# Local attention: outputs of two items in one PSUM tile, scores in alternation with transpositions

## The chip, the cores and the metric

The kernel runs on one core of a Trainium2 chip. The metric is the device time of one execution in microseconds (us); the median of several runs counts. Engines are called by the names of the profile: PE is TensorE (matmuls and transpositions), DVE is VectorE, ACT is ScalarE, SP is the engine whose queue issues the DMAs here.

## The reference

Three steps follow one another: local attention with a few global tokens, then two MLPs. There are 4 batches of 8 heads of width 64, 512 local and 32 global positions.

```python
s_g = scale * q_g @ k_all.T;  out_g = sm(s_g) @ v_all        # 32 global queries see all 544 keys
s_ll = where(abs(i - j) <= 32, scale * q_l @ k_l.T, -1e9)    # local queries: a band of +-32
a_l = sm(concat([scale * q_l @ k_g.T, s_ll]))                # and the 32 global keys
out_l = a_l @ concat([v_g, v_l])
x = out.transpose(0, 2, 1, 3).reshape(B * S, 512)            # 2176 tokens
h = x @ w_in;  x = where(h >= 1, h, where(h <= -1, 0, (h + 1)**2 / 4)) @ w_out    # 512 -> 2048 -> 512
y = ((x @ w_a) * (x @ w_b)) @ w_out2                         # 512 -> 1536 -> 512
```

## The kernel before

**Tiles.** The 2048 local tokens are 16 blocks of 128, the 128 global ones a 17th. `TILES` groups them by three into tiles 0 to 4; tile 5 has block 15 and the global block. The first MLP takes one tile (384 columns) after the other.

**Attention items.** A `Local` item is one block and one pair of heads; there are 64, four for each block, listed block by block. An item goes through three steps, called atoms here. *Score*: `s_pe` computes 128x224 scores for each of two heads on PE, `s_post` masks them and takes the minimum on DVE (L199, two instructions), then exponentials with sums on ACT (L203, two). For blocks 6 and up, `prep` first splits queries and keys into a high and a low part (L166 to L169, tiles qs, kh and kl with one buffer). `norm` adds an epsilon, takes the reciprocal and scales one head on DVE (L207, L208, L210), the other on ACT (L209). *Transposition*: `t_pe` transposes the weights in four PE transpositions into a PSUM tile tp, `t_post` copies it to SBUF on ACT (L220, tile pt, two buffers). *Output*: `v_pe` multiplies with v (L226; the trace has eight instructions an item) into a PSUM tile o of 128 columns, `v_post` copies that into the row xraw on DVE (L230). The eight `Glob` items have the same steps.

**Order.** `att_atoms` is a generator that writes this order. In round k it issues loads, the score of item k, `norm` of item k-1, the transposition of item k-2 and the output of item k-3, and hands control back (`yield`) after each of the three atoms:

```python
it.s_pe() ... it.s_post()          # item k
items[k - 1].norm()
it.t_pe(); it.t_post()             # item k-2
it.v_pe(); it.v_post()             # item k-3
```

Tile 0's attention runs alone at the start, with one conversion of a weight slice (`W1.step`) after every `START_ATOMS` = 8 atoms. After that, attention of tile t+1 is woven into the first MLP of tile t. The MLP has 16 units a tile, each with two halves of 12 matmuls: `h_unit` (the hidden layer, PSUM tile hp) and, two units later, `x_unit` (the output, PSUM tile acc). After each half a credit grows by `rate`, and an atom is issued for every whole credit, so `rate = 3.0 * n_items / 31` spreads three atoms an item over the 32 halves (over 28 in tile 4, up to `GLOB_END`). What is left at the end of a tile is issued at once. Three `Gap` entries after tile 1 empty the pipeline, since blocks from 6 on need memory that is free only when tile 1's MLP begins.

While tile 0's MLP runs, two weight slices a unit are converted and split (L97 to L100, L107, L108). `x_split` (L405, L406) splits the rows of a tile before its first `h_unit`.

**What else sets the order.** The code is written for a framework that plans each engine's order at build time from priorities (the written order) and estimated durations: an instruction that is ready can pass one that is not. On the chip each engine then runs its list in that order and waits where it must.

**Buffers.** PSUM has eight banks: four with the tag "h" (hp, scores s, and for tiles from 1 on also tp and o), four with "acc" (acc; in the first stage tp, o and the filling matmuls). v has three buffers, e four, pt two.

## Time and profile before

| what | value |
|---|---|
| median of 3 runs | 957.22 us (955.91 to 957.30) |
| the profiled execution: its time | 954.88 us |
| the profiled execution: its span, first to last instruction | 953.1 us |
| mean granted PE clock | 0.996 |
| busy share of the span | PE 97%, DVE 76%, ACT 57% |
| matmuls and weight loads | 5964 each |

All times in the trace are of the one profiled execution, counted from the start of its span. Busy time is the time in which an engine worked on something. Matmuls overlap in the pipeline and their ends are modelled, so for PE the distance from start to start says more than a duration. An engine that waits costs time only where it is the limit at that point.

### The profile page before, as it was taken

How to read it: one execution, taken by the hardware profiler on the slowest of the kernel's cores; microseconds unless marked ns; L12 is line 12 of the kernel's file. 1: busy time of each engine (PE TensorE's matmuls, PEld its weight loads, DVE VectorE, ACT ScalarE, POOL GpSimd, SP SyncE). 2: the span in 40 equal slices, each digit the busy share in tenths (PEclk: the TensorE clock that was granted, in tenths of full speed). 3: DMA queues.
4: the chain of work that ended last, by engine and by line, in shares of the span. 5: the costliest groups of instructions: out<-in, count | busy, mean ns of one | idle time of the engine just before them, and what ended most of it. 6: DMA issues, size and time to landing. Idle time of an engine off the chain costs nothing.

```text
span 953.1 us, 16713 instructions
## 1 busy us (share of the span) xinstructions
PE 926.9 (97%) x5964; PEld 840.3 (88%) x5964; DVE 728.2 (76%) x1881; ACT 539.6 (57%) x1293; POOL 0.7 (0%) x7
## 2 busy tenths in 40 slices
PE   7898988999999999999999999999999999999997
PEld 5587777999999999987889999999999999999996
DVE  6799999888877877764348968888896666877663
ACT  8867767666666666654445555555654444654441
POOL 0000000000000000000000000000000000000000
PEclk9899999999999999999999999999999999999999
DMA  7455546444544444333454323321241111131201
GB/s 238 148 189 182 182 164 188 156 133 142 178 142 132 160 156 147 96 120 104 134 194 149 94 79 112 98 69 48 72 147 45 45 45 48 44 121 56 57 12 56
DMA packets 55843, 111.49 MB, mean 117 GB/s; under 512 B 6864, under 2 KB 23376, under 8 KB 55760
## 3 DMA queue, kind: packets, MB, share of 16 engines
q1 hardware_dynamic: 55616, 110.26, 36.4%
q8 instruction: 47, 0.77, 0.3%
q14 instruction: 36, 0.29, 0.1%
q10 hardware_dynamic: 144, 0.17, 0.1%
HBM read 95.20 MB, written 15.20 MB: 116 GB/s over the span
## 4 chain that ended last, share of the span: by engine, by line
PE 84%; DVE 9%; ACT 3%; DMA 2%; issue 1%; SPq 0%; ACTq 0%; DVEq 0%
PE hp L423 6%; PE hp L425 6%; PE hp L424 6%; PE acc L423 6%; PE acc L424 5%; PE acc L425 5%; PE pb L580 5%; PE pb L581 5%; PE py L645 5%; PE pb L578 5%; PE py L646 5%; PE py L644 5%; PE px L578 4%; PE px L581 4%; PE px L580 4%; PE o L226 3%
## 5 line engine op out<-in xcount | busy, mean ns | idle before, releaser
L423 PE MATMUL hp<-xh,w 128*128 128x384 f32 (+1 forms) x384 | 131.5, 342 | 5.4 <-ACT xh L405 2.1
L423 PE MATMUL acc<-g,w 128*128 128x384 f32 (+1 forms) x384 | 132.0, 344 | 4.2 <-ACT g L708 3.6
L424 PE MATMUL acc<-g,w 128*128 128x384 f32 (+1 forms) x384 | 127.1, 331 | 0.0
L425 PE MATMUL hp<-xl,w 128*128 128x384 f32 (+1 forms) x384 | 126.5, 330 | 0.0
L424 PE MATMUL hp<-xh,w 128*128 128x384 f32 (+1 forms) x384 | 126.0, 328 | 0.0
L425 PE MATMUL acc<-g,w 128*128 128x384 f32 (+1 forms) x384 | 125.0, 330 | 0.0
L107 ACT ACTIVATE w<-wt 128x512 fp32r<-128x512 f32 (+1 forms) x116 | 64.9, 564 | 70.8 <-PE pb L581 44.9
L580 PE MATMUL pb<-w 128*128 128x384 f32 (+1 forms) x288 | 94.7, 329 | 0.0
L581 PE MATMUL pb<-w 128*128 128x384 f32 (+1 forms) x288 | 94.3, 327 | 0.0
L578 PE MATMUL pb<-w 128*128 128x384 f32 (+1 forms) x288 | 93.7, 325 | 0.0
L704 DVE SCALAR_TENSOR_TENSOR m<-hp,r 128x384 f32<-128x384 f32 (+1 forms) x96 | 51.1, 532 | 49.5 <-ACT r L703 49.4
L703 ACT ACTIVATE r<-hp,half 128x384 f32<-128x384 f32 (+1 forms) x96 | 53.4, 556 | 61.1 <-PE hp L425 60.6
L423 PEld LDWEIGHTS hp<-xh,w 128*128 128x128 f32 x384 | 72.9, 190 | 12.8 <-issue 3.4
L423 PEld LDWEIGHTS acc<-g,w 128*128 128x128 f32 x384 | 72.4, 189 | 12.5 <-issue 5.3
L645 PE MATMUL py<-w,g 128*128 128x512 f32 x204 | 80.8, 396 | 0.0
L646 PE MATMUL py<-w,g 128*128 128x512 f32 x204 | 80.7, 396 | 0.0
L644 PE MATMUL py<-w,g 128*128 128x512 f32 x204 | 79.6, 390 | 0.0
L108 DVE TENSOR_TENSOR w<-wsum,w 128x256 fp32r<-128x256 f32 (+1 forms) x108 | 54.6, 507 | 29.6 <-ACT w L107 29.6
L424 PEld LDWEIGHTS acc<-g,w 128*128 128x128 f32 x384 | 72.6, 189 | 1.6 <-issue 1.0
L425 PEld LDWEIGHTS acc<-g,w 128*128 128x128 f32 x384 | 72.2, 188 | 1.7 <-issue 1.2
L708 ACT ACTIVATE g<-m 128x384 fp32r<-128x384 f32 (+1 forms) x96 | 48.3, 503 | 44.6 <-DVE m L705 43.9
L425 PEld LDWEIGHTS hp<-xl,w 128*128 128x128 f32 x384 | 72.9, 190 | 0.7 <-DVE xl L406 0.5
(112 smaller groups left out, 2131.6 us busy)
## 6 DMA issues: line engine op xcount, KB each, us to landing
wt<-wd SPq DMA_DIRECT2D x72, 256.0 KB, 2.7
qkd<-in_qkd_dram SPq DMA_DIRECT2D x40, 352.0 KB, 3.1
wraw<-in_w1i_dram SPq DMA_DIRECT2D x16, 512.0 KB, 3.5
wraw<-in_w1o_dram SPq DMA_DIRECT2D x16, 512.0 KB, 4.0
v<-in_vw_dram SPq DMA_DIRECT2D x64, 112.0 KB, 2.8
wraw<-in_w2a_dram SPq DMA_DIRECT2D x12, 512.0 KB, 3.7
wraw<-in_w2b_dram SPq DMA_DIRECT2D x12, 512.0 KB, 4.0
wd<-wt SPq DMA_DIRECT2D x24, 256.0 KB, 2.2
```

The costliest lines, as they stand in the source:

```text
L107: nc.scalar.activation(hi, src, AF.Copy)
L108: nc.vector.tensor_tensor(lo, src, f32(hi), ALU.subtract)
L423: nc.tensor.matmul(acc, whi, xhi, start=first, stop=False)
L424: nc.tensor.matmul(acc, wlo, xhi, start=False, stop=False)
L425: nc.tensor.matmul(acc, whi, xlo, start=False, stop=last)
L578: nc.tensor.matmul(out[:, :n], w[:, 0, r], hi[:, c, :n], start=start and c == 0, stop=False, skip_group_check=True)
L580: nc.tensor.matmul(out[:, :n], w[:, 1, r], hi[:, c, :n], start=False, stop=False, skip_group_check=True)
L581: nc.tensor.matmul(out[:, :n], w[:, 0, r], lo[:, c, :n], start=False, stop=k in (1, 5, 6) and c == 1, skip_group_check=True)
L644: nc.tensor.matmul(a, gh[:, c], w[:, 0], start=f == 0, stop=False)
L645: nc.tensor.matmul(a, gh[:, c], w[:, 1], start=False, stop=False)
L646: nc.tensor.matmul(a, gl[:, c], w[:, 0], start=False, stop=f == NF2 - 1)
L703: at["act"] = nc.scalar.activation(r[:, :W], hp[:, :W], AF.Relu, bias=half, scale=0.5 / W_UP).ins
```

## The change

Items are listed in pairs: of a tile's three blocks, the items of the first two with the same heads stand next to each other, and the third block's four items make two pairs. `Local.v_pe` gets its PSUM target from outside, and `v_post` goes. A round of the generator now handles two items in five atoms: score k, transposition k-2, score k+1, transposition k-1, then both outputs k-2 and k-1 into one PSUM tile of 2 x 128 columns. Where the two blocks are neighbours in a row, one copy of 256 columns empties it, else two of 128. The loads, `prep` and `norm` are spread over the round; the loads of v stand just ahead of the outputs. There are two gaps after tile 1 and two ahead of the global items, which keep the old order in a loop of their own. The pace falls from 3.0 to 2.6 atoms an item.

```diff
@@ -219,15 +219,11 @@
             self.pt = ap.tile([P, 4, P], F32, name="pt", tag="pt", bufs=2)
             nc.scalar.activation(self.pt[:KC], self.tp[:KC], AF.Copy)
 
-        def v_pe(self):
-            self.o = ps.tile([P, P], F32, name="o", tag=self.tag)
+        def v_pe(self, o):
             for c in range(2):
                 for h in range(2):
-                    nc.tensor.matmul(self.o[64 * h:64 * h + 64], self.v[:, c, 64 * h:64 * h + 64],
+                    nc.tensor.matmul(o[64 * h:64 * h + 64], self.v[:, c, 64 * h:64 * h + 64],
                                      self.pt[:KC, 2 * c + h], start=c == 0, stop=c == 1)
-
-        def v_post(self):
-            nc.vector.tensor_copy(xraw_cur[self.t][self.p][:, self.j * P:(self.j + 1) * P], self.o)
 
     class Gap:
         stk = False
@@ -323,59 +319,114 @@
     items = []
     ends = {}
     for t, blks in enumerate(TILES):
-        for j, blk in enumerate(blks):
-            if blk == GLOB:
-                continue
+        loc = [(j, blk) for j, blk in enumerate(blks) if blk != GLOB]
+
+        for n in range(0, len(loc) - 1, 2):
             for p in range(NPAIR):
-                items.append(Local(t, j, blk, p))
+                items += [Local(t, *loc[n], p), Local(t, *loc[n + 1], p)]
+        if len(loc) % 2:
+            items += [Local(t, *loc[-1], p) for p in range(NPAIR)]
+        if t == 1:
+            ends[t] = len(items)
+            items += [Gap(), Gap()]
+            continue
+        if GSCHED.get(t):
+            items += [Gap(), Gap()]
         for b in GSCHED.get(t, []):
             for q in range(2):
                 items.append(Glob(b, q))
         ends[t] = len(items)
-        if t == 1:
-            items += [Gap(), Gap(), Gap()]
 
     def att_atoms():
         n = len(items)
-        nl = nv = npr = 0
+        ng = next(i for i, it in enumerate(items) if isinstance(it, Glob))
+        cnt = {"l": 0, "v": 0, "p": 0}
         started = set()
-        for k in range(n + 3):
-            while nl < min(k + (2 if nl < n and isinstance(items[nl], Glob) else 3), n):
-                if items[nl].stk and "k" not in gp:
+
+        def loads(k):
+            while cnt["l"] < min(k, n):
+                if items[cnt["l"]].stk and "k" not in gp:
                     break
-                items[nl].load()
-                nl += 1
-            while npr < min(k + 1, nl):
-                items[npr].prep()
-                npr += 1
-            while nv < min(k, n):
-                items[nv].load_v()
-                nv += 1
-            if k < n and items[k].t is not None:
-                it = items[k]
-                it.s_pe()
-                if k < WARM_ITEMS:
-                    it.fill()
-                it.s_post()
-            if 1 <= k <= n and items[k - 1].t is not None:
+                items[cnt["l"]].load()
+                cnt["l"] += 1
+
+        def loads_v(k):
+            while cnt["v"] < min(k, n):
+                items[cnt["v"]].load_v()
+                cnt["v"] += 1
+
+        def preps(k):
+            while cnt["p"] < min(k, cnt["l"]):
+                items[cnt["p"]].prep()
+                cnt["p"] += 1
+
+        def score(k):
+            items[k].s_pe()
+            if k < WARM_ITEMS:
+                items[k].fill()
+            items[k].s_post()
+
+        def turn(k):
+            items[k].t_pe()
+            items[k].t_post()
+
+        def outs(a, b):
+            if a.t not in started:
+                started.add(a.t)
+                new_xraw(a.t)
+            o = ps.tile([P, 2, P], F32, name="o", tag=a.tag)
+            x = xraw_cur[a.t]
+            a.v_pe(o[:, 0])
+            b.v_pe(o[:, 1])
+            if a.p == b.p and b.j == a.j + 1:
+                nc.vector.tensor_copy(x[a.p][:, a.j * P:(a.j + 2) * P], o.rearrange("p a b -> p (a b)"))
+            else:
+                for i, it in enumerate((a, b)):
+                    nc.vector.tensor_copy(x[it.p][:, it.j * P:(it.j + 1) * P], o[:, i])
+
+        for k in range(0, ng, 2):
+            now = k < ng and items[k].t is not None
+            old = k >= 2 and items[k - 2].t is not None
+            loads(k + 2)
+            preps(k + 1)
+            if now:
+                score(k)
+                loads(k + 3)
+                preps(k + 2)
+                yield k, 0
+            if old:
+                turn(k - 2)
+                yield k, 1
+            if now:
+                score(k + 1)
+                items[k].norm()
+                loads(k + 4)
+                preps(k + 3)
+                yield k, 0
+            if old:
+                turn(k - 1)
+                yield k, 1
+            loads_v(k)
+            if old:
+                outs(items[k - 2], items[k - 1])
+                yield k - 1, 2
+            if now:
+                items[k + 1].norm()
+        for k in range(ng, n + 3):
+            loads(k + 2)
+            loads_v(k)
+            if k < n:
+                score(k)
+            if ng + 1 <= k <= n:
                 items[k - 1].norm()
-            while npr < min(k + 2, nl):
-                items[npr].prep()
-                npr += 1
-            if k < n and items[k].t is not None:
+            if k < n:
                 yield k, 0
-            if 2 <= k <= n + 1 and items[k - 2].t is not None:
-                it = items[k - 2]
-                it.t_pe()
-                it.t_post()
+            if ng + 2 <= k <= n + 1:
+                turn(k - 2)
                 yield k, 1
-            if 3 <= k and items[k - 3].t is not None:
-                it = items[k - 3]
-                if isinstance(it, Local) and it.t not in started:
-                    started.add(it.t)
-                    new_xraw(it.t)
-                it.v_pe()
-                it.v_post()
+            if ng + 3 <= k:
+                items[k - 3].v_pe()
+                items[k - 3].v_post()
                 yield k - 3, 2
 
     att = att_atoms()
@@ -759,7 +810,7 @@
                     gp["p"] = es_att.enter_context(tc.tile_pool(name="gp", bufs=1, reuse_waits="tile"))
                 if f == 0 and t + 1 < nt:
                     n_items = ends[t + 1] - done["n"]
-                    rate = 3.0 * n_items / (2 * (GLOB_END if t == nt - 2 else NF1) - 1)
+                    rate = 2.6 * n_items / (2 * (GLOB_END if t == nt - 2 else NF1) - 1)
                     credit = 0.0
                 if (t, f) == (nt - 2, GLOB_END):
                     for _ in att:
```

## Rows read from the trace of the kernel before

**Rows 1.** The page, part 1: busy time, share of the span and instructions of each engine.
```profile
PE 926.9 (97%) x5964; PEld 840.3 (88%) x5964; DVE 728.2 (76%) x1881; ACT 539.6 (57%) x1293; POOL 0.7 (0%) x7
```

**Rows 2.** Stages: length, then busy us of PE, PEld, DVE, ACT, POOL; clock; DMA.
```profile
5.00:38.00 33.00, 27.58 (x221) 18.58 (x220) 28.71 (x134) 31.57 (x97) 0.00 (x0) 0.98 0.76 234
38.00:138.00 100.00, 91.63 (x536) 77.05 (x537) 95.19 (x235) 68.16 (x148) 0.00 (x0) 0.97 0.48 160
138.00:160.00 22.00, 19.22 (x107) 15.83 (x106) 19.72 (x58) 16.02 (x44) 0.00 (x0) 1.00 0.67 212
...
234.00:321.00 87.00, 87.00 (x578) 81.69 (x577) 70.35 (x199) 56.30 (x143) 0.00 (x0) 1.00 0.46 148
```

**Rows 3.** PE's waits: us, times, longest; 38 to 138, last line 160 to 234 us.
```profile
PE acc L423 <- ACT g L708: 3.0, 2, 1.7
...
PE hp L423 <- ACT pt L220: 0.2, 1, 0.2
```

**Rows 4.** Timeline of PE: start us, length us, instruction; one output of eight matmuls.
```profile
290.10 0.34 PE L425 MATMUL hp<-xl,w 128*128 128x384 f32 x1
290.37 0.66 PE L226 MATMUL o<-pt,v 112*64 112x128 f32 x8
...
291.24 0.34 PE L424 MATMUL acc<-g,w 128*128 128x384 f32 x1
291.41 0.34 PE L425 MATMUL acc<-g,w 128*128 128x384 f32 x1
```

**Rows 5.** Timeline of PE, 134 to 136 us: two outputs in a row.
```profile
134.06 0.34 PE L425 MATMUL hp<-xl,w 128*128 128x384 f32 x1
134.33 1.09 PE L226 MATMUL o<-pt,v 112*64 112x128 f32 x16
...
135.63 0.33 PE L424 MATMUL hp<-xh,w 128*128 128x384 f32 x1
```

**Rows 6.** Timeline of PE and ACT: two transpositions and their copies to pt.
```profile
287.75 0.60 PE L216 MATMUL tp<-ident,e 128*112 128x128 f32 x4
...
288.38 0.60 ACT L220 ACTIVATE pt<-tp 112x512 f32<-112x512 f32 x1
...
301.52 0.60 PE L216 MATMUL tp<-ident,e 128*112 128x128 f32 x4
...
304.44 0.57 ACT L220 ACTIVATE pt<-tp 112x512 f32<-112x512 f32 x1
```

**Rows 7.** Groups of instructions, DVE: copies of o (128 columns) and of acc (384).
```profile
L230 DVE COPY xraw<-o 128x128 f32<-128x128 f32 x64 | 18.2, 285 | 9.4 <-PE o L226 9.4
...
L730 DVE TENSOR_SCALAR x<-acc 128x384 f32<-128x384 f32 x8 | 4.4, 556 | 0.1
```

**Rows 8.** Timeline of ACT, 30 to 33 us: one item's steps.
```profile
31.05 0.47 ACT L203 ACTIVATE e<-e,mn 128x224 f32<-128x224 f32 x1
...
31.52 0.47 ACT L209 ACTIVATE e<-e,sm 128x224 f32<-128x224 f32 x1
31.89 0.58 ACT L220 ACTIVATE pt<-tp 112x512 f32<-112x512 f32 x1
32.37 0.66 ACT L97 ACTIVATE wt<-wraw 128x512 f32<-128x512 f32 x1
```

**Rows 9.** Groups of DVE, 38 to 138 us: count, busy us, mean ns.
```profile
L199 DVE CUSTOM_DVE_ANT_0 e<-s,masks 128x224 f32<-128x224 f32 x18 | 6.7, 384 | 0.1
...
L210 DVE TENSOR_SCALAR e<-e,sm 128x224 f32<-128x224 f32 x9 | 3.0, 331 | 0.0
...
L207 DVE TENSOR_SCALAR sm<-sm 128x2 f32<-128x2 f32 x9 | 1.5, 165 | 0.0
```

**Rows 10.** Tile v, 11 to 38 us: its loads' time to landing.
```profile
DMA to landing us min/median/max: 2.1/2.8/4.2
```

**Rows 11.** Start of the hidden layer: PE's first matmul; clock before 44 us.
```profile
37.77 0.69 PE L423 MATMUL hp<-xh,w 128*128 128x384 f32 x1 [2.14 <-ACT xh L405]
...
37.00:44.00 7.00, 6.23 (x16) 4.56 (x16) 3.74 (x9) 4.03 (x10) 0.00 (x0) 0.51 0.19 76
```

## The prediction

> **What bounds the kernel now.** I read the busy shares first, then the stages, then TensorE's waits, then single instructions. TensorE (PE) is busy for 926.9 of 953.1 us [rows 1], but that counts overlapping and stretched matmuls, so the stages have to say more. By stage [rows 2] three limits follow one another. From 5 to 38 us, attention of the first tile alone, ScalarE (ACT) is busy 31.57 of 33 us. From 38 to 138 us, where the first MLP runs on tile 0 while its 32 weight slices are converted, VectorE (DVE) is busy 95.19 of 100. From 160 us until the attention ends in tile 4's MLP PE is the limit; from 234 to 321 it has no gap, 87.00 of 87 us. Attention of the next tile is woven between groups of 12 matmuls there, so every nanosecond that attention takes from PE's stream is on the path, and no other engine is near its limit (there DVE has 70, ACT 56 of 87). The waits agree [rows 3]: in the DVE stretch PE waits for ACT's g for 3.0 us, the longest of its waits there, and from 160 to 234 us once, for 0.2 us; from 234 to 408 us the view has no wait at all. In tile 5's MLP and the second MLP nothing of the change runs.
>
> **Outputs of two items back to back.** In the PE stretch the price of a group is read from start to start. Matmuls of 384 columns follow each other every 0.17 us (291.24 to 291.41). With eight output matmuls between them, the last before and the second after stand 290.10 to 291.24 = 1.14 us apart [rows 4]. Two plain steps would be 0.35, so a single output costs 0.79; part of that lies outside the outputs themselves, as in the 0.27 from the last matmul to the first output (290.10 to 290.37), where a plain step takes 0.17. The trace has one place where two outputs happen to stand together, sixteen matmuls: 134.06 to 135.63 = 1.57 [rows 5], less 0.35 is 1.22. So a pair saves 2 x 0.79 - 1.22 = 0.36 us. Scores and transpositions stay 64 each, one group each as before, so they save nothing.
>
> How many pairs count: 64 items make 32 pairs. The 12 pairs of tiles 0 and 1 run where ACT or DVE is the limit, so their PE time is covered and counts 0; without that cover they would add 12 x 0.36 = 4.3. Tiles 2, 3 and 4 have six pairs each and tile 5 two: 20 pairs, at most 20 x 0.36 = 7.2 us.
>
> Not each pair stays whole. Before, an output used a transposition that was a whole item old. Now the second output follows its own transposition after one group of 12 matmuls. ACT must have copied the transposed tile (pt) by then: counted from the start of the transpositions, their 0.60 and 12 x 0.17 make about 2.6 us, or 3.1 if the first output's eight go ahead meanwhile. One of the quickest copies ends at 288.98 for transpositions that start at 287.75, 1.2 us; one of the slowest at 305.01 for 301.52, 3.5 us [rows 6]. I went through all 24 between 234 and 408 us: 18 end within 3.1 us. Where pt is late, the framework's planned order puts the next unit's matmuls ahead of the second output and the pair costs what it cost before; nothing is lost but the gain. So 15 of 20 pairs: 15 x 0.36 = **-5.4 us**. Bounds: 0 and -7.2.
>
> **The wider evacuation.** 20 pairs are neighbours in a row and get one 256-column copy; the other 12 keep two copies. No row has that copy. From PSUM 128 columns take 285 ns and 384 take 556 (row of the x copies) [rows 7], so 256 lies near 285 + 135 = 420, and a wide one saves 150 ns of DVE. From 160 us on DVE is covered by PE: 0. Tiles 0 and 1 have four each; the four of the DVE stretch count 0.6 us, the four of the ACT stretch nothing.
>
> **The first 138 us.** The first stage ends with the outputs of item 11. Before, the loop had by then scored 15 items, normalised 14 and transposed 13; now 14, 13 and 12. ACT's steps [rows 8] start 0.46 apart for each of two exponentials, 0.37 for the scaling and 0.48 for the pt copy: 0.92 + 0.37 + 0.48 = 1.8 us that leave the ACT stretch. They come back in the next one, as DVE work: two masked reductions of 0.38, two small normalising steps of 0.17 and a scaling of 0.33 [rows 9], 1.4 us. The weight slice that was converted as fourth inside the loop (one per 8 atoms, of fewer atoms) is now converted as fourth just behind it: same work, moved past the first split of x on ACT and DVE, 0 here. Sum: -1.8 + 1.4 - 0.6 = **-1.0 us**. Bounds: -3 where the lighter first stage also starts the matmuls earlier, and +2 for two things. Each load keeps its count, but SP's order changes: in a round v comes behind two loads of queries and keys, whose buffers are free by then. The second v load of a pair can now start only when the previous pair's outputs are done; v lands in 2.1 to 4.2 us there [rows 10], and a pair's share of the 33 us is 5.5, so the load just fits. And the clock: just ahead of the first hidden matmuls PE idles for 2.14 us, and from 37 to 44 us the granted clock is 0.51 [rows 11], nearly all of it at the lower level (1.2 GHz). Seven us at about half rate cost some 3.4. I leave it as it is.
>
> **Start of tile 1's MLP and the pace.** From 138 to 160 us PE is busy 19.22 of 22 [rows 2]: the doubled loads and splits of the first tile-2 items press on DVE and ACT. Atoms are now handed out at 2.6 x 14 / 31 = 1.17 per half unit instead of 3.0 x 15 / 31 = 1.45, so they press less. I take **-0.5** out of a possible -2.8; a loss I bound at +0.5. In the other stages 30 atoms at 1.006 per half unit (2.6 x 12 / 31) end by the 30th of 32, so none is left for a flush. The global items keep their order; their first load is traced just ahead of the first global score instead of three atoms earlier, and SP is free well before: 0.
>
> **Sum.** -5.4 - 1.0 - 0.5 = -6.9 us. The profiled execution took 954.9 us around its 953.1 of span, so 948.0 for it. The median of the runs shown is 957.2, 2.3 above it; the forecast is 957.2 - 6.9 = **950.3 us**. About 0.2% (1.9 us) is what a measurement of this kernel tells from no change.
>
> **The rivals.**
> *A larger gain.* All 20 pairs stay whole (1.8 more), the low-clock stretch moves into the ACT-bound stage (up to 3.4) or the start of tile 1 clears (2.3): two of these give 945 to 946. For it: all three are in rows. Against: none follows from the edit by itself.
> *The change does not do what it says.* pt is late nearly always and the pairs are split: only the front's 1.5 us and a few pairs remain, 954.5 to 957. For it: 6 of 24 copies are late today, and now exponentials, splits and pt of neighbouring items crowd two groups. Against: ACT has slack, 56 of 87.
> *Slower, by a chain in the first stage.* pt has two buffers. ACT cannot copy the next transposition before both outputs of the pair are through, and these wait for the pair's second pt. If the planned order puts the next score behind the outputs, ACT, the limit there, stands while PE runs both outputs (1.22) and a score and DVE its reduction (0.38), with only one scaling (0.37) as cover: 1.2 us and the score, by estimate 1.5, in each of six pairs, +9 us, so 950.3 + 9 = 959 to 960. It decides at whether scores pass waiting outputs in PE's order. Against it: in this trace PE's order is already adaptive, with transpositions and scores out of the written order.
> *Slower, by the shared bank.* Both outputs lie in one PSUM tile, so DVE cannot empty the first while the second is computed; a bank is held some 0.45 us longer, plus 0.13 for the wider copy. If each pair held up the next hidden tile by that, 20 x 0.58 = 11.6, and the kernel would take about 962. Against it: PE waits for no bank between 234 and 408 us, and there is one tile fewer per pair. The Trainium skill's page Perfetto Trace Analysis, section Optimizing Tensor Performance, says that independent matmul groups should rotate through different PSUM banks so that the evacuation of one overlaps the next group's matmuls; by that rule this rival is the outcome, and the trace, with no such wait, does not bear it out.
>
> **How the numbers follow.** The forecast (947 to 954) gets 0.51, the larger gain 0.16, split pairs 0.20, the first-stage chain 0.10, the bank 0.03. Faster by over 0.2% (below 955.3) is the forecast, the larger gain and a third of the split case: 0.74. Slower (above 959.1) is both last rivals: 0.13. The rest, 0.13, is the same. The range takes in the larger gain and most of the split case: 944.5 to 957.5.
>
> **What would show it.** In the changed profile, from 234 to 408 us: PE without waits, most output groups of 16, each with 1.2 us for its place, and two stages of about 85 instead of 87 us. The step is wrong if groups of 8 prevail, or if PE waits for ACT pt ahead of outputs. The first hidden matmul should start at about 36 us (now 37.8); a first stage longer than 33 us with ACT idle for PE's scores is the chain. PE waits for DVE's copy of o would be the bank. If the time falls though 16-groups are rare, the sum was right by luck.

## The result, and the profile after

The changed kernel took 961.77 us, the median of nine runs (958.73 to 965.19), against 957.22 for nine runs of the kernel before beside it (954.97 to 964.02): a ratio of 1.0057, 95% interval 1.0036 to 1.0078. It is slower by about 4.5 us where 6.9 less was forecast. The profiled execution took 959.32 us and has a span of 957.54 us, 4.5 more than the 953.06 before, so the two profiles hold nearly all of the difference.

The busy shares say nothing of it. Part 1 of the page of the changed kernel, to be set beside [rows 1]:

```profile
PE 924.2 (97%) x5964; PEld 842.4 (88%) x5964; DVE 726.6 (76%) x1860; ACT 540.3 (56%) x1294; POOL 0.7 (0%) x7
```

PE is busy for 2.7 us less in a span that is 4.5 us longer, so it stands idle more. The stages of the changed kernel (length, then busy us of PE, PEld, DVE, ACT and POOL with instruction counts, granted clock, DMA share, GB/s), to be read against [rows 2]:

```profile
5.00:38.00 33.00, 29.40 (x220) 19.61 (x219) 26.87 (x122) 30.61 (x94) 0.00 (x0) 0.99 0.69 217
38.00:138.00 100.00, 89.40 (x531) 75.76 (x530) 94.12 (x235) 67.72 (x148) 0.00 (x0) 0.97 0.51 163
138.00:160.00 22.00, 17.95 (x99) 15.62 (x98) 19.37 (x53) 14.62 (x38) 0.00 (x0) 1.00 0.67 200
160.00:234.00 74.00, 70.82 (x485) 66.60 (x485) 59.82 (x170) 49.40 (x126) 0.00 (x0) 1.00 0.49 155
234.00:321.00 87.00, 86.03 (x582) 82.40 (x581) 70.53 (x196) 56.84 (x144) 0.00 (x0) 1.00 0.47 148
```

Before the change the fourth of these stretches was

```profile
160.00:234.00 74.00, 73.75 (x490) 68.30 (x490) 61.46 (x177) 49.78 (x128) 0.00 (x0) 1.00 0.48 153
```

From 138 to 234 us, where PE had 19.22 of 22 ([rows 2]) and 73.75 of 74 busy us, it now has 17.95 and 70.82; from 234 on it is no longer gapless. PE's waits over the whole span (us in total, times, longest), to be read against [rows 3], name what it stands for:

```profile
PE o L225 <- ACT pt L220: 8.1, 13, 1.2
PE acc L474 <- ACT g L759: 7.0, 6, 2.4
PE s L186 <- DMA qk<-in_qk_dram: 5.2, 3, 3.8
```

The first line is new: outputs (line 225 now) wait for the copy of their own transposition, 13 times. In the kernel before, no line of this view has an output that waits for pt. One such place on PE, start, length, instruction, and in brackets the idle time ahead of it with what ended it:

```profile
261.34 0.34 PE L476 MATMUL acc<-g,w 128*128 128x384 f32 x1
261.61 0.66 PE L225 MATMUL o<-pt,v 112*64 112x128 f32 x8
262.97 0.66 PE L225 MATMUL o<-pt,v 112*64 112x128 f32 x8 [0.71 <-ACT pt L220]
263.56 0.44 PE L474 MATMUL hp<-xh,w 128*128 128x384 f32 x1
```

And ACT in the same stretch:

```profile
261.48 0.48 ACT L209 ACTIVATE e<-e,sm 128x224 f32<-128x224 f32 x1 [0.72 <-DVE sm L208]
261.87 0.56 ACT L754 ACTIVATE r<-hp,half 128x384 f32<-128x384 f32 x1
262.33 0.58 ACT L220 ACTIVATE pt<-tp 112x512 f32<-112x512 f32 x1
```

The pair stays together in PE's list. The first output ends, the second stands there and waits until ACT, which has the scaling of the next item and the hidden layer's Relu ahead of it, has copied pt. The twelve matmuls of the next group stand behind it. ACT was not short of time here: the transposition was through at 259.6 us, and ACT itself stood idle for 0.72 us, as long as PE's 0.71, because the scaling that is ahead of the copy in its list waited for DVE's sm.

To see where the time went I measured each tile's MLP from its first hidden-layer matmul to that of the next tile (192 of them a tile), in us. The other rows of this table belong to the experiments below; each was one profiled execution, and the ratio is that of all its runs to runs of the kernel before on the same chip.

| kernel | first hidden matmul | tile 0 | tile 1 | tile 2 | tile 3 | tile 4 | ratio (95% interval) |
|---|---|---|---|---|---|---|---|
| before | 37.77 | 100.31 | 95.72 | 86.95 | 87.11 | 97.68 | 1 |
| changed | 36.19 | 103.04 | 96.63 | 86.34 | 86.25 | 101.27 | 1.0057 (1.0036 to 1.0078) |
| no gaps | 41.66 | 100.13 | 95.75 | 86.35 | 86.26 | 99.05 | 1.0034 (1.0013 to 1.0055) |
| late outputs | 36.85 | 100.20 | 98.51 | 84.84 | 84.84 | 98.68 | 0.9956 (0.9932 to 0.9980) |
| two tiles | 36.01 | 102.41 | 94.84 | 86.14 | 86.09 | 101.05 | 1.0039 (1.0014 to 1.0064) |
| old front | 41.58 | 99.05 | 94.65 | 86.31 | 86.26 | 102.05 | 1.0024 (1.0010 to 1.0039) |
| late, no gaps | 38.17 | 97.37 | 98.26 | 84.84 | 84.84 | 97.69 | 0.9963 (0.9943 to 0.9982) |
| the same, old front | 37.35 | 99.22 | 95.95 | 84.84 | 84.84 | 97.69 | 0.9943 (0.9922 to 0.9965) |
| pace 3.0 | 42.95 | 103.15 | 97.70 | 91.45 | 91.39 | 99.31 | 1.0153 (1.0128 to 1.0177) |
| new front alone | 42.00 | 101.05 | 96.83 | 86.95 | 87.11 | 97.69 | 1.0042 (1.0024 to 1.0060) |
| four qk buffers | 36.80 | 102.25 | 95.79 | 86.30 | 86.27 | 101.59 | 1.0038 (1.0023 to 1.0053) |
| late, no gaps, four, slower | 36.35 | 98.99 | 97.33 | 85.75 | 84.84 | 97.79 | 0.9957 (0.9938 to 0.9977) |
| late, no gaps, old front, slower | 36.89 | 100.39 | 92.76 | 85.75 | 84.84 | 97.62 | 0.9934 (0.9918 to 0.9950) |
| before, slower | 37.56 | 99.14 | 94.67 | 89.34 | 87.11 | 97.89 | 1.0031 (1.0010 to 1.0051) |

In the changed kernel the first stage is 1.6 us shorter, tile 0's MLP 2.7 longer, tile 1's 0.9 longer, tiles 2 and 3 are 0.6 and 0.9 shorter, and tile 4's is 3.6 longer; the rest takes 0.3 more. The sum is 4.5, from the unrounded values.

### The profile page after: what moved, and what is told of

It is laid out like the page before. It is cut to its first block, busy times and chain, and to the rows that moved or that the text cites. A ratio compares the mean times of both kernels' runs of the same rounds, so it can differ in the third digit from the quotient of the medians.

```text
span 957.5 us, 16692 instructions
## 1 busy us (share of the span) xinstructions
PE 924.2 (97%) x5964; PEld 842.4 (88%) x5964; DVE 726.6 (76%) x1860; ACT 540.3 (56%) x1294; POOL 0.7 (0%) x7
## 4 chain that ended last, share of the span: by engine, by line
PE 73%; DVE 14%; ACT 6%; DMA 3%; issue 3%; ACTq 0%; SPq 0%; DVEq 0%
PE pb L631 5%; PE pb L632 5%; PE py L696 5%; PE pb L629 5%; PE py L697 5%; PE py L695 5%; PE hp L474 5%; PE hp L476 4%; PE hp L475 4%; PE acc L474 4%; PE acc L476 4%; PE acc L475 4%; PE px L629 4%; PE px L632 4%; PE px L631 4%
## 5 line engine op out<-in xcount | busy, mean ns | idle before, releaser
L108 DVE TENSOR_TENSOR w<-wt,w 128x512 fp32r<-128x512 f32 (+1 forms) x116 | 70.1, 605 | 6.4 <-ACT w L107 5.1
```

The source lines that it names most:

```text
L108: nc.vector.tensor_tensor(lo, src, f32(hi), ALU.subtract)
```

## The experiments

My theory after the two profiles had three parts: second outputs wait for pt (tiles 1 to 5), the gaps ahead of the global items empty the attention's pipeline (tile 4's stage), and the new order costs in the first two tiles. The rivals were the shared PSUM tile, and that one of these parts explains the others.

### No gaps ahead of the global items

```diff
-        if GSCHED.get(t):
-            items += [Gap(), Gap()]
...
-            if ng + 2 <= k <= n + 1:
+            if k <= n + 1:
                 turn(k - 2)
                 yield k, 1
+            if k == ng + 1:
+                outs(items[ng - 2], items[ng - 1])
+                yield ng - 1, 2
```

Only the first global load is let through early. The pace of tile 4's MLP is 3.0 an item, which is 1.33 atoms a half over the items without gaps; the changed kernel hands out 1.35 over items and gaps.

> The changed kernel without the two gaps ahead of the global items: tile 5's last two transpositions and its last pair of outputs are woven between the first global scores, and the pace in tile 4's MLP is what it was. Theory (the gaps empty the attention's pipeline, then the global scores run one behind the other at the pace of their key loads, and one score and one transposition more fall into this stage): tile 4's stage, 101.27 us in the changed kernel and 97.68 before, returns to 98 to 99 and the three groups of sixteen score matmuls that took 1.65 us take 1.05 again, so about 2.8 us less, 959.0, ratio to before near 1.002. Rival (the loss in that stage comes from the pairs themselves, outputs waiting for pt): stage 101 as it is, 961.8, ratio 1.005.

Tile 4's stage fell from 101.27 to 99.05 and the ratio to 1.0034. The matmuls of the global scores (sixteen for each load) in the changed kernel, with all that runs between them left out:

```profile
429.24 1.12 PE L263 MATMUL sg<-kg 64*32 64x272 f32 x16
433.34 1.72 PE L263 MATMUL sg<-kg 64*32 64x272 f32 x16
438.04 1.70 PE L263 MATMUL sg<-kg 64*32 64x272 f32 x16
```

and with the gaps away, the MLP's matmuls left out:

```profile
424.69 1.12 PE L263 MATMUL sg<-kg 64*32 64x272 f32 x16
427.95 0.60 PE L216 MATMUL tp<-ident,e 128*112 128x128 f32 x4
430.57 1.12 PE L263 MATMUL sg<-kg 64*32 64x272 f32 x16
431.62 0.65 PE L216 MATMUL tp<-ident,e 128*112 128x128 f32 x4
434.32 1.09 PE L225 MATMUL o<-pt,v 112*64 112x128 f32 x16
437.64 1.12 PE L263 MATMUL sg<-kg 64*32 64x272 f32 x16
```

In the changed kernel the scores start at 429 instead of 418 us and then follow every 4 to 5 us, one load behind the other (the tile of keys has one buffer, and its loads take 3.1 us to land). Three of the groups take 1.65 us from the first of the sixteen to what follows, instead of 1.05. Their starts show how: where four of them had stood 7 ns apart and the next four 233 ns behind, they now follow after 7, 221, 32 and 197 ns. Why they are spread is not shown; another planned order inside the group would do it. With tile 5's last steps woven between, the first three groups start 6 to 7 us apart and are short again. That confirms the theory for 2.2 of the 3.6 us. PE itself idles little in this stage, 1.0 us against 0.4 before; the price of the gaps is mostly these longer groups: summed from start to start, the global scores took 10.21 us of its stream in the changed kernel, 8.41 before and 8.68 without gaps. The remaining 1.4 lie, by the same sums, mostly in the hidden layer's matmuls (36.30 instead of 35.31 us before) and in one more score (0.88 instead of 0.44); both went with late outputs, below.

### Outputs one round later

```diff
             if now:
                 score(k)
...
+            if older:
+                outs(items[k - 4], items[k - 3])
+                yield k - 3, 2
             if old:
                 turn(k - 2)
...
-            if old:
-                outs(items[k - 2], items[k - 1])
-                yield k - 1, 2
```

The loads of v move behind the first transposition, and tile 1 is followed by four gaps at an unchanged pace. These two go with the new place of the outputs and were not tried alone; PE's waits in the changed kernel name no load of v.

> The changed kernel with the outputs of a pair one round later, just behind the next-but-one pair's first score, so that their transpositions are a round old; same buffers. Theory (second outputs stand in PE's order before their pt is copied, and PE waits for it, 8.1 us in 13 waits): those waits go to under 1 us, the stages of tiles 1 to 3 become shorter, 96.6 to 95.5, 86.3 to 85.3 and 86.3 to 85.5, tile 4's by 1 where a gap still empties the pipeline; some 4 to 6 us in all, 956 to 958, ratio 1.000. Rival (the waits are only where the lateness of ACT or DVE shows, and move to the next score or to the hidden layer's matmuls): sum of PE's waits as before within 2 us, time 960 to 962.

The ratio fell by a whole per cent, from 1.0057 to 0.9956: this kernel is faster than the one before. That is nearly twice the gain expected (4 to 6 us, ratio 1.000); the two profiles hold 6.0 us of it. Tiles 2 and 3, length, busy us of PE, PEld, DVE, ACT, POOL, clock, DMA:

```profile
234.00:321.00 87.00, 87.00 (x590) 83.97 (x590) 72.19 (x201) 58.09 (x147) 0.00 (x0) 1.00 0.46 148
321.00:408.00 87.00, 87.00 (x592) 83.92 (x591) 70.65 (x196) 56.29 (x143) 0.00 (x0) 1.00 0.44 142
```

PE is gapless again and gets through 590 matmuls where it got through 578 [rows 2]. A pair on PE:

```profile
261.04 0.34 PE L479 MATMUL acc<-g,w 128*128 128x384 f32 x1
261.31 1.09 PE L225 MATMUL o<-pt,v 112*64 112x128 f32 x16
262.34 0.44 PE L477 MATMUL hp<-xh,w 128*128 128x384 f32 x1
```

Tiles 2 and 3 take 84.84 us each, together 4.38 less than before for twelve pairs, so a pair saves 0.365 us. In tile 2, summed from start to start, the outputs take 6.14 us of PE's stream where the changed kernel took 7.65, and every other kind of matmul takes the same in both within 0.01; these 1.51 are the whole difference of the stage, 86.34 to 84.84. Waits for pt ahead of outputs are 2.1 us in all, and neither lies behind 138 us:

```profile
PE o L225 <- ACT pt L220: 2.1, 2, 1.1
```

Two expectations on stages missed too: tile 4's stage fell by 2.6 us, not 1, and tile 1's stage rose to 98.5 instead of falling. There PE waits 1.9 and 1.4 us for DVE's split of the queries. A likely reason, not tried alone, is that the four gaps leave the pipeline to be filled again in a stretch, 138 to 160 us, in which DVE is busy 19.69 of 22 us.

### Two PSUM tiles for a pair

```diff
-            o = ps.tile([P, 2, P], F32, name="o", tag=a.tag)
-            a.v_pe(o[:, 0])
-            b.v_pe(o[:, 1])
...
+            for it in (a, b):
+                o = ps.tile([P, P], F32, name="o", tag=a.tag)
+                it.v_pe(o)
+                nc.vector.tensor_copy(x[it.p][:, it.j * P:(it.j + 1) * P], o)
```

> The changed kernel, but each of a pair's outputs has its own PSUM tile of 128 columns and its own copy, as before the change; they still stand back to back. Theory (the shared tile costs nothing; what costs is the order): 961 to 963, the 20 additional copies cost at most 0.6 us in the stretch where DVE is the limit; PE waits for pt as in the changed kernel, 7 to 9 us. Rival (the shared bank of the prediction: the evacuation of the first output cannot lie beside the second): PE's waits get shorter and the time falls by 3 us or more, to 958 or less.

PE's wait for pt is what it was, 8.0 us in 14 places:

```profile
PE o L225 <- ACT pt L220: 8.0, 14, 1.5
```

The ratio is 1.0039, and its interval overlaps that of the changed kernel; tiles 2 and 3 are 0.2 us shorter each. Separate tiles leave the waits for pt and a kernel that is still slower than the one before, so the shared bank is not the cause. That separate tiles give something, by the two intervals up to some 5 us, these runs can't exclude. The rule of the Trainium skill that the prediction weighed (page Perfetto Trace Analysis, section Optimizing Tensor Performance: rotate independent groups through different banks) has the outcome's sign but not its mechanism: with two banks the same waits are there.

### The old order in tiles 0 and 1, and the new order there alone

Old front (tiles 2 to 5 as changed, the pace 3.0 in tile 0's MLP), cut:

```diff
+        nf = ends[1]
+        for k in range(nf + 3):
...
+            if k < nf:
+                score(k)
+            if 1 <= k <= nf:
+                items[k - 1].norm()
+            if 2 <= k <= nf + 1:
+                turn(k - 2)
+            if k >= 3:
...
+                it.v_pe(o)
-        for k in range(0, ng, 2):
+        for k in range(nf + 2, ng, 2):
```

> Tiles 0 and 1 with the items, rounds and pace of the kernel before (score, transposition, output of three successive items), tiles 2 to 5 as changed. Theory (of the 4.5 us that the span grew, 1.15 arose before tile 1's MLP and 0.9 in it, from the crowding of DVE and ACT while weights are converted): tile 1's MLP starts at 138.0 to 138.3 instead of 139.2, first hidden matmul at 37.8 instead of 36.2, the later stages as in the changed kernel; 960.0 to 961.0, ratio 1.003 to 1.004. Rival (the front gains, since its ACT-bound stage is 1.6 us shorter, and the rest of tile 0's stage is chance): tile 1's MLP starts at 139.5 or later and the time stays at 961.8 or rises.

New front alone is the complement, with the loop of pairs up to the gaps of tile 1 and the old loop behind it:

```diff
-        for k in range(0, ng, 2):
+        for k in range(0, nf + 2, 2):
...
+        for k in range(nf + 3, n + 3):
```

> The changed order in tiles 0 and 1 alone (pairs, rounds of five atoms, both outputs in one tile, pace 2.6 in tile 0's MLP); the items of tiles 2 to 5, the global ones and the three gaps as before the change. Theory (the front as changed costs, by what old order in tiles 0 and 1 gave back: 1.0057 less 1.0024): ratio 1.001 to 1.004, that is 1 to 4 us slower than before, tile 0's MLP stage 102 to 103 instead of 100.3, tile 1's about 96. Rival (the prediction's term, 1.0 us gained before tile 1's MLP and 0.5 at its start): ratio 0.998 to 0.999.

The old front took the ratio down to 1.0024, the new front alone put it at 1.0042. The two shifts, 0.0033 and 0.0042, agree within their intervals, and both are on the side of a cost: some 3 to 4 us, where the prediction had a gain of 1.5. How it comes about can't be read from one row of the table, since the first hidden matmul of single executions with the same front comes up to 7 us apart; that is also why the old front's tile 1 starts at 140.6 us in its profile and not at the 138 expected (its clock was 0.50 from 30 to 37 us). In the profile of the new front alone, length, busy us of PE, PEld, DVE, ACT, POOL, and the granted clock as the third number from the end:

```profile
20.00:23.00 3.00, 1.62 (x15) 1.00 (x14) 1.72 (x9) 2.64 (x9) 0.00 (x0) 1.00 0.79 247
23.00:26.00 3.00, 3.00 (x18) 1.81 (x16) 1.78 (x9) 2.21 (x8) 0.00 (x0) 0.63 0.28 78
26.00:38.00 12.00, 12.00 (x56) 7.51 (x55) 6.61 (x32) 6.82 (x22) 0.00 (x0) 0.50 0.44 124
```

and PE just ahead of it:

```profile
20.53 0.66 PE L225 MATMUL o<-pt,v 112*64 112x128 f32 x8
22.57 0.65 PE L186 MATMUL s<-qk 64*128 64x224 f32 x4 [1.38 <-DMA qk<-in_qk_dram]
```

PE waits 1.38 us for a load of queries and keys, then the granted clock falls to 0.50, its lower level (1.2 GHz), and stays there to 38 us and beyond; the first hidden matmul comes at 42.0. In the changed kernel's own profile the same wait was 1.18 us at 22.27, and the clock stayed at 1.00.

### Four buffers for queries and keys

```diff
-                self.qk = sp["q"].tile([P, P + KW], F32, name="qk", bufs=3)
+                self.qk = sp["q"].tile([P, P + KW], F32, name="qk", bufs=4)
```

> The changed kernel with four instead of three buffers for the queries and keys of tiles 0 and 1; nothing else. In the changed first stage PE waits 1.2 to 2.0 us at about 21 us for a load of queries and keys, SP's queue stands 10 to 13 us (5 before) until a score has freed a buffer, and in several runs the granted clock is 0.5 from then on to about 38 us. Theory (scores now come in twos, so three buffers make the load of the next pair late; with four, the load of an item goes out one score earlier): no wait of PE for such a load between 12 and 38 us, SP's wait for scores under 4 us, no fall of the clock before the first hidden matmul, which starts at 35 to 36.5 us; fewer runs with a mean clock under 0.993; ratio 1.002 to 1.004 instead of 1.0057. Rival (the buffers are not what the first stage lacks; the second outputs' wait for pt paces it): the first stage as in the changed kernel, ratio 1.0057 within 0.001.

SP's waits in the first stage, 10 to 38 us, in the changed kernel (us in total, times, longest):

```profile
SPq L157 <- PE s L186: 8.1, 10, 1.3
```

and with four buffers:

```profile
SPq L157 <- PE s L186: 3.9, 4, 1.8
```

The loads wait half as long for scores (SP's waits for outputs, behind which it refills v, rose from 6.9 to 9.4 us, so part of its standing only moved), PE's longest wait for such a load fell from 1.2 to 0.6 us (none was expected), the clock stays at 1.00 to 37 us, and the first hidden matmul comes at 36.80, a little later than expected. All six runs have a mean granted clock of 0.996 or more; of the changed kernel's nine runs six had 0.992 or less. The ratio of 1.0038 is where the theory put it, but its interval overlaps that of the changed kernel, and in the profile tile 1's MLP starts at 139.05 us, as good as unchanged from 139.23. So three buffers are shown to make the loads late; that they cost the median time is likely and not settled.

### The pace

```diff
-                    rate = 2.6 * n_items / (2 * (GLOB_END if t == nt - 2 else NF1) - 1)
+                    rate = 3.0 * n_items / (2 * (GLOB_END if t == nt - 2 else NF1) - 1)
```

> The changed kernel with the pace of before alone, 3.0 atoms an item instead of 2.6. Theory (the order inside a pair's round is the cause, not how fast the atoms are handed out): PE's waits for pt ahead of outputs stay at 6 to 10 us, ratio 1.004 to 1.008, as the changed kernel's 1.0057; at most the start of tile 1's MLP suffers, up to 1 us. Rival (the slower pace delays the attention, and with it the copies to pt): waits for pt under 4 us, ratio 1.003 or less.

Both missed: the ratio is 1.0153, and outputs wait 11.6 us for pt. Part of it is the first stage, which in this execution ran at a clock of 0.79 from 5 to 38 us (6.8 us later than the changed kernel's at the first hidden matmul). The rest is in tiles 2 and 3, 5.1 us longer each than with 2.6. One place in tile 2 holds 3.9 us of it. PE:

```profile
280.29 0.33 PE L476 MATMUL acc<-g,w 128*128 128x384 f32 x1
282.65 0.66 PE L225 MATMUL o<-pt,v 112*64 112x128 f32 x8 [2.02 <-ACT pt L220]
...
283.90 0.52 PE L476 MATMUL acc<-g,w 128*128 128x384 f32 x1
284.22 0.52 PE L474 MATMUL acc<-g,w 128*128 128x384 f32 x1
```

and the windows around it, same columns as above:

```profile
280.00:282.00 2.00, 0.63 (x3) 0.31 (x3) 1.34 (x5) 1.28 (x4) 0.00 (x0) 1.00 0.52 152
282.00:284.00 2.00, 1.35 (x11) 1.18 (x12) 1.66 (x4) 1.12 (x3) 0.00 (x0) 0.86 0.96 343
284.00:286.00 2.00, 2.00 (x8) 2.00 (x7) 0.44 (x1) 0.00 (x0) 0.00 (x0) 0.50 0.51 184
```

At 3.0 the pair's outputs come right behind its second transposition, with no group of twelve matmuls between, the wait for pt grows to 2.02 us, and behind it the clock goes to its lower level for about 3 us: matmuls follow every 0.32 us instead of 0.17. Here the planned order did split the pair (three matmuls stand between its two outputs), and PE waited all the same. So the slower pace is a part without which the change costs a per cent more.

### Both edits together, and the best version

Late outputs and no gaps in one kernel:

> Both single edits together: a pair's outputs one round later, and no gaps ahead of the global items (tile 5's last transpositions and pair outputs woven between the first global scores). Theory (two separate costs, pt waits in tiles 1 to 5 and the emptied pipeline in tile 4's stage, so they add up): tile 4's stage 96 to 97 (98.7 with late outputs alone, 99.1 without gaps alone, 101.3 with neither, 97.7 before), stages of tiles 2 and 3 84.8 as with late outputs alone; ratio to before 0.993 where late outputs alone gave 0.9956, some 948.5. Rival (what the gaps cost is a wait that late outputs have already taken away or that comes back as waits for the global keys): ratio 0.9955 again, stage 98.5 or more.

Tile 4's stage came to 97.69, what it was before the change, so the two edits do address two costs (98.68 and 99.05 with one, 101.27 with neither). But they don't add up: the single gains of 2.59 and 2.22 would give 96.5, 97.69 is not the 96 to 97 expected, and the ratio, 0.9963 where 0.993 was expected, does not differ from that of late outputs alone; 1.0 us in one stage is not seen through the scatter. The same with the old order and pace in tiles 0 and 1:

> The same as the run with both edits, but tiles 0 and 1 in the order and pace of the kernel before, so that pairs exist only in tiles 2 to 5, where TensorE is the limit. Theory (pairs gain only where TensorE is the limit, and in tiles 0 and 1 they cost through bunched work on ACT and DVE and through the longer refill after tile 1): tile 1's stage 94.5 to 95.5 where late outputs alone had 98.5, tile 0's near 100; ratio 0.989 to 0.991, 2 to 4 us below the run with both edits. Rival (with the outputs a round later the front costs nothing any more, and its 98.5 was chance): no difference between the two runs within 1 us.

Ratio 0.9943, tile 1's stage 95.95: the direction of the theory, of smaller size, and the intervals overlap. In that stage one wait stood out, and what followed it:

```profile
158.00:160.00 2.00, 0.36 (x3) 0.04 (x1) 1.97 (x7) 1.35 (x5) 0.00 (x0) 1.00 0.35 127
160.00:162.00 2.00, 1.83 (x9) 1.58 (x10) 1.90 (x7) 0.91 (x4) 0.00 (x0) 0.85 0.92 261
162.00:164.00 2.00, 2.00 (x8) 2.00 (x7) 1.56 (x8) 1.70 (x6) 0.00 (x0) 0.50 0.63 188
```

```profile
PE s L179 <- DVE qs L168: 1.7, 1, 1.7
```

PE waits 1.7 us for DVE's split of the queries, and the clock falls again. So the last versions slow the pace in tile 1's MLP only, here against the run just above:

```diff
-                    n_items = ends[t + 1] - done["n"]
+                    n_items = ends[t + 1] - done["n"] - (t == 1)
```

> The run with both edits and the old order in tiles 0 and 1, with the slower pace in tile 1's MLP alone (1.09 instead of 1.17 atoms a half). Theory: the one wait of 1.7 us at 160 us and the 3 us at half clock behind it go; tile 1's stage 92.5 to 94.5 instead of 95.95, ratio 0.990 to 0.993 where the pace before gave 0.9943. Rival (the wait moves to another score): stage 95.5 to 96.5, ratio 0.994 to 0.995.

The best version: 948.51 us beside 954.97 for the kernel before, ratio 0.9934. Tile 1's stage is 92.76; the wait is 1.2 us now and the clock stays at 1.00, while tile 2's stage is 0.9 longer. Both kernels, the one before and the changed one, are beaten; from the run just above it is not told apart by its interval, and the ratio lies just outside the 0.990 to 0.993 expected. The same pace with the new front and four buffers did not get there:

> Late outputs and no gaps ahead of the global items, with four buffers for queries and keys in the first stage and a slightly slower pace in tile 1's MLP (2.6 x 13 / 31 = 1.09 instead of 1.17 atoms a half). Theory: with both edits alone the kernel stood at 0.9963, and in its tile 1 stage (98.3 us) PE waits 1.9 and 1.4 us for DVE's split of the queries, the second of them followed by some 3 us at half clock; a slower pace gives DVE 8% more time between these splits, so the longest of these waits falls under 1 us and the stage to 95 to 97; the first stage loses its waits for loads. Ratio 0.990 to 0.993. Rival (these waits are set by DVE's total work there, not by the pace): stage 98 again, ratio 0.9955 or more.

0.9957, tile 1's stage 97.33: its longest wait for the split stayed at 1.9 us, so the rival holds here: the slower pace alone does not remove it. Last, the slower pace in the kernel before, with no pairs:

```diff
-                    n_items = ends[t + 1] - done["n"]
+                    n_items = ends[t + 1] - done["n"] - 3 * (t == 1)
```

> The kernel before the change with one edit: in tile 1's MLP atoms are handed out at 3.0 x 12 / 31 = 1.16 per half instead of 1.45; no pairs. It tells what of the best version's gain in tile 1's stage (92.8 us instead of 95.7) is the pace and what the pairs. Theory (six pairs give 6 x 0.36 = 2.2 us, the pace less than 1): tile 1's stage 94.8 to 95.8, ratio 0.999 to 1.001. Rival (the pace alone): stage 93.5 or less, ratio 0.998 or less.

Tile 1's stage fell by 1.05, but what was left over made tile 2's 2.39 longer; the ratio is 1.0031, slower than either expected. So pace alone gains nothing, and the best version's gain rests on the pairs: 2.96 us in tile 1's stage (of which the pace may have a share) and 3.47 in tiles 2 and 3.

## Why the prediction was wrong

**The price of a pair was right.** 2 x 0.79 - 1.22 = 0.36 us was read from one place in the trace [rows 4, 5]; twelve pairs that do not wait save 4.38 us, 0.365 each. As the prediction said, part of it lies not in the outputs but in the matmuls around them. The wide copy was priced right too: 256 columns took 417 ns, against some 420.

**Where the miss lies.** Stage by stage, forecast and measured in the two profiles: up to tile 1's MLP -1.0 and +1.15, tile 1's stage -2.1 and +0.91, tiles 2 and 3 together -3.2 and -1.47, tile 4's -0.5 and +3.59, the rest 0 and +0.3. The first failed step below accounts for the 1.8 us of tiles 2 and 3 and is at work in the other stages too; the second, which overlaps with it, made the loss in tile 4's.

**The step that failed: "Where pt is late, the planned order puts the next unit's matmuls ahead of the second output and the pair costs what it cost before; nothing is lost but the gain."** The rows for it [rows 6] were rightly read: a copy takes 1.2 to 3.5 us and the second output follows about 3 us behind its transposition. Even the count of late ones was near: 20 of 24 copies end within 3.1 us in the changed kernel, and 4 of the 12 pairs in tiles 2 and 3 had to wait. But the plan is made from estimated durations and fixed at build time. It kept these pairs together (what it estimated for pt is not on record), and PE, which runs its list in order, waited. The cost of a late pt was therefore not 0 but the wait and a little more, since a pair that waits 0.71 us takes 2.15 us of PE's stream instead of 1.22. In tiles 2 and 3 twelve pairs gained 1.47 us instead of 4.38. The prediction named the sign to look for (PE waiting for ACT's pt ahead of outputs) and it came, 8.1 us. Moving the outputs by one round, same buffers and same pairs, brought the gain back in full in these two stages: there the cause is shown.

**The second step that failed: "The global items keep their order; their first load is traced just ahead of the first global score instead of three atoms earlier, and SP is free well before: 0."** This cost 3.6 us in tile 4's stage. The step weighed the load of the first global item and SP, not the two gaps ahead of it: they drain the pipeline, so that global scores, which had tile 5's last steps between them, then run at the pace of their single-buffered loads, and three of these groups take 1.65 us of PE's stream instead of 1.05. One score and one transposition more also moved into that stage. Removing the gaps took back 2.2, late outputs alone 2.6, both 3.6.

**"The first 138 us", -1.0.** The first stage did become shorter, by 1.6 us, the first hidden matmul came at 36.19 (about 36 was forecast). The return in the next stage was mis-sized: 2.7 us, not 0.8, so tile 1's MLP starts 1.15 later. Over all profiles with the changed front it starts at 138.4 to 146.1 (median of six 140.5), with the old order and pace there at 136.6 to 140.6 (median of five 137.3), with the new front and late outputs at 135.3 to 137.1 (three). So with late outputs the forecast gain seems to be there, though the three groups overlap. That the same wait for pt took it is likely and not shown: from 38 to 138 us PE is busy 89.40 instead of 91.63 us at the same mean clock, 0.97, and its waits that name pt are 3.2 us instead of 1.0. The bound of +2 for SP's queue was put in the right place, with a wrong reason: not v (SP stood 6.9 us for outputs in that stage, 6.8 before), but the loads of queries and keys (8.1 us for scores, 4.0 before).

**"Start of tile 1's MLP", -0.5.** That tile's whole stage, in which six pairs should have gained as well, became 0.9 longer, although the pace was slower. From 138 to 160 us, a stretch that now begins 1.2 us ahead of that stage, PE is busy 17.95 instead of 19.22 us; it waited 1.3 and 0.7 us for g, and later in the stage 1.2 us twice for pt.

**The rivals.** The measured time, 961.77, is what the shared bank was priced at (962), but its mechanism was not there: PE's waits name DVE's copy of o nowhere, and with two tiles the waits for pt are unchanged. So the number agrees by luck. The chain in the first stage (959 to 960) did not lengthen that stage in the profile either. "The change does not do what it says" was nearest in tiles 2 and 3, with the difference that pairs are not split but wait. The sign of the forecast failed because no rival had a second output that waits in PE's order, a wait that the change itself adds: the question of what stands behind it on PE was asked for the first stage only.

## What to carry to other kernels

When two steps are put side by side to save a switch, look at what the second one needs and how old that is at its new place: a gain of 0.36 us a pair was real, and a round more of distance decided between 0.6% slower and 0.4% faster. A build-time order does not move out of the way of a wait that its estimates don't foresee, so price a late operand by the wait and by all that stands behind it. Gaps and paces around a reordered loop are changes of their own; here the gaps were worth some 2 us and the pace some 9.

## What the runs showed of the hardware

A short wait of PE can be followed by a lower granted clock, also in the midst of dense work. Behind 2.02 us (pace 3.0) and 1.71 us (old front, late) it was 0.50 for some 3 us, behind 1.38 us in the first stage 0.50 for 12 us and more. But behind 1.24 us at 176 and 1.19 us at 213 us in the changed kernel it stayed at 1.00, and with the slower pace and four buffers it fell behind 1.21 us:

```profile
160.00:162.00 2.00, 0.70 (x3) 0.19 (x2) 1.94 (x7) 1.56 (x6) 0.00 (x0) 1.00 0.59 207
162.00:164.00 2.00, 1.81 (x10) 1.81 (x11) 1.97 (x8) 1.94 (x5) 0.00 (x0) 0.89 0.83 217
164.00:166.00 2.00, 2.00 (x8) 1.56 (x9) 1.94 (x8) 1.58 (x6) 0.00 (x0) 0.50 0.38 149
```

The plainest case is one place in three kernels: ahead of a score at 146 to 148 us PE waits 1.9 us for the same split. With late outputs, alone or without gaps, the clock is 1.00 in the 4 us from 146 on; with the slower pace and four buffers it is 0.57. So the length of the wait alone does not tell whether the clock falls. The price of a wait of 1 to 2 us lies, by estimate, between a little more than itself (0.93 us for the 0.71 at 262 us) and more than twice itself (the first hidden matmul at 42.0 instead of 36.2 us behind the 1.38). Clock and time also go together in the scatter: of the sixteen runs of the kernel before that stood beside the last experiment, the five with a mean granted clock of 0.997 or more took 952.85 to 954.56 us, the three with 0.992 or less 956.90 to 960.97.
